# Query products on quarter tiles of TensorE: one head and 64 tokens each, in an attention and Fourier-mix kernel on one core

## The chip, the core and the metric

The kernel runs on one core of a Trainium2 chip. Its five engines work side by side, each with an instruction queue of its own: TensorE multiplies matrices and writes into PSUM banks, VectorE (DVE), ScalarE (ACT) and GpSimd (POOL) work on elements, SyncE (SP) issues transfers. The metric is the device time of the whole program in microseconds. Before the change the median of three runs is 1039.37 us (1037.9 to 1042.61).

## What is computed

Eight batches of 576 tokens, 8 heads of 64 columns. First an attention without a token-by-token matrix, then a Fourier mix with a two-layer network:

```python
q_s = exp(q - max(q, head's columns));  q_s /= sum(q_s, head's columns) + 1e-9
k_s = exp(k - max(k, tokens));          k_s /= sum(k_s, tokens) + 1e-9
kv  = einsum('bhsd,bhse->bhde', k_s, v)          # a 64x64 table a head
x   = einsum('bhsd,bhde->bhse', q_s, kv)         # heads joined to 512 columns
u   = x + real(fft(fft(x, axis=tokens), axis=columns))
out = u + relu(norm(u) @ w_ch1) @ w_ch2          # 512 -> 2048 -> 512
```

The step that matters here is the second product with the table, `q_s` times `kv`. Everything is float32.

## The kernel before

The program is one list of steps, each with a time in a plan made by hand. The steps are sorted by that time and issued in that order, so every engine's queue has a fixed order. A batch's attention is planned among the matmuls of the network of an earlier batch: TensorE works on the network (lines 1371, 1468, 1498, 1587, products with fewer multiplications by Strassen's rule), and now and then takes a few products of the attention.

**Tables.** Heads come in four pairs, `r` = 0 to 3. The table of a pair is kept as one square of 128x128 with the two 64x64 heads on its diagonal and zeros elsewhere, and two further columns P and P+1, one for each head, that hold ones in the rows of that head: 130 columns a pair, in the tile `kvr`. There are two such tiles, for even and odd batches. `keys.scale` (lines 717 to 726) fills the diagonal from the product of keys and values, once a pair; `prepare` (line 652) writes the ones, by four small memsets on GpSimd.

**Own tokens.** Of a batch's 576 tokens, 512 form four tiles of 128. `own_exp` takes the exponential and lays the tile out turned: 128 rows are the columns of a pair of heads, 128 columns are tokens. `own_times_kv` (line 781) multiplies: for each pair of heads the turned queries are the weights (128x128) and the table is streamed (130 columns). Two pairs share a PSUM bank, two banks a tile. The columns P and P+1 of the result are the sums of a head's queries. `inverse` takes their reciprocals, and two multiplications on VectorE, one a bank, divide and move the result to SBUF. There are 24 such tiles in batches 2 to 7.

**Shared tokens.** The other 64 tokens of two batches share one tile, `F`. It is folded along the tokens for the Fourier transform, and `t_times_kv` (line 996) multiplies 128 of its rows by 128 columns of the same tables, four products into one bank, without the sums. ScalarE copies the bank to two places, and three VectorE instructions fold it. There are 6 such tiles in batches 2 to 7.

**Banks.** All these products, those of keys and values (line 716), and the blocks of the transform (lines 1088 to 1116) take PSUM banks in turn from three, with the name `acc`. A product that asks for a bank waits until whoever reads the bank's former content is done.

In batches 0 and 1 the query products are made by other functions, which are left as they are: `q_times_kv` (line 957), and `t_times_kv` as well.

Of the kernel before, what the change touches and what calls it, by code (L numbers as in the profile page):

```python
# [40 lines left out]
F32 = mybir.dt.float32  # L41
# [97 lines left out]
class _Block:  # L139
    def __init__(self, ctx, tc, q, kT, v, w1, w2, ft, cd, out):  # L140
        self.nc, self.tc = tc.nc, tc
        self.q, self.kT, self.v, self.w1, self.w2, self.out = q, kT, v, w1, w2, out
        self.ft_dram, self.cd_dram = ft, cd
        nc = self.nc
        pool = lambda name, **kw: ctx.enter_context(tc.tile_pool(name=name, bufs=1, **kw))
        self.const, self.work, self.small = pool("const"), pool("work"), pool("small")
        self.ps = pool("ps", space=bass.MemoryType.PSUM)
        self.dram = pool("dram", space=bass.MemoryType.DRAM)
        c = self.const
        self.ident = c.tile([P, P], F32, name="ident")  # L150
        make_identity(nc, self.ident[:])
        self.eps = c.tile([P, 1], F32, name="eps")
        nc.gpsimd.memset(self.eps[:], LN_EPS)
        self.kvr = []
        for b in range(2):
            t = c.tile([P, NR, P + 2], F32, name=f"kvr{b}")
            nc.gpsimd.memset(t[:], 0.0)
            self.kvr.append(t)

        self.sn = []  # L160
        for i in range(2):
            t = c.tile([P, NN], F32, name=f"sn{i}")
            nc.gpsimd.memset(t[:], 0.0)
            self.sn.append(t)

        self.ZT = c.tile([P, KT, P], F32, name="ZT")

        self.Zr, self.ZTr = c.tile([P, HD], F32, name="Zr"), c.tile([P, P], F32, name="ZTr")
        for t in (self.Zr, self.ZTr):
            nc.gpsimd.memset(t[:], 0.0)  # L170
        self.kb = c.tile([P, NR, 4, NC * Q], F32, name="kb")
        kb = self.kb[:].rearrange("p r g s -> p (r g s)")
        self.kss = [kb[:, i * NC * P:(i + 1) * NC * P].rearrange("p (c n) -> p c n", n=P) for i in range(NR)]
        self.vt = c.tile([P, NC, 2 * P + 2], F32, name="vt")

        self.T, self.F = c.tile([P, 2 * NR, 4, NT], F32, name="T"), c.tile([P, 2 * NR, P], F32, name="F")
        nc.gpsimd.memset(self.T[:], 0.0)

        self.ones = c.tile([P, NR, H], F32, name="ones")
        nc.gpsimd.memset(self.ones[:], 0.0)  # L180
        for h in range(2):
            nc.gpsimd.memset(self.ones[64 * h:64 * h + 64].rearrange("p r h -> p (r h)")[:, h::H + 2], 1.0)

        self.sign = c.tile([P, 1], F32, name="sign")
        nc.gpsimd.memset(self.sign[:], -1.0)
        nc.gpsimd.memset(self.sign[0:Q + 1], 1.0)
        d = self.dram
        self.w1s = [d.tile([P, 7, HD], F32, tag=f"w1s{p}", name=f"w1s{p}", bufs=1) for p in range(NP)]
        self.w2s = d.tile([7, P, NP, HD], F32, tag="w2s", name="w2s", bufs=1)

        self.w2d = d.tile([P, len(DEEP), GT], F32, tag="w2d", name="w2d", bufs=1)
        self.plan, self.base = [], {}
        for at in range(1, B + 1):
            self.base[at] = len(self.plan)
            self.plan += [self.w1s[p][:].rearrange("p a n -> p (a n)") for pair in PAIRS for p in pair]
            one = lambda m: self.w2s[WB_AT[m]].rearrange("p a n -> p (a n)")
            first = self.first_deep(at)
            self.plan += [one(m) for m in (ORDER if at == 1 else (1, 2) if at == B else (1,))]
            if at > 1:
                for i in range(first, len(DEEP), 4):  # L200
                    self.plan.append(self.w2d[:, i:min(i + 4, len(DEEP)), :].rearrange("p a n -> p (a n)"))
            if at == B:
                self.plan.append(one(4))

        self.big = c.tile([P, 3 * NF * D], F32, name="big")
        self.fifth = self.big[:, 3 * NF * D - 5 * P:3 * NF * D - P].rearrange("p (r n) -> p r n", n=P)
        nc.gpsimd.memset(self.fifth[0:64], 0.0)
        part = lambda i: self.big[:, i * NF * D:(i + 1) * NF * D].rearrange("p (f n) -> p f n", n=D)
        self.w1sb, self.w2sb, self.h0 = part(0), part(1), part(2)
        self.ft = c.tile([P, 4 * NM], F32, name="ft")  # L210
        self.cd = c.tile([P, 5 * QD + 1], F32, name="cd")
        self.xs, self.live, self.stream = {}, {}, {}
        self.turns = 0
        self.eo, self.unT, self.Z = {}, {}, {}
        self.unused = None

        self.later = []

        self.words = [self.work.tile([P, 2, D], F32, tag=n, name="words", bufs=k) for n, k in (("xs", 2), ("x", 4), ("x", 4))]
# [433 lines left out]
    def prepare(self):  # L653


        G = self.nc.gpsimd
        for t in self.kvr:
            for h in range(2):
                G.memset(t[64 * h:64 * h + 64, :, P + h:P + h + 1], 1.0)
        for col in (0, 2 * P + 1):  # L660
            G.memset(self.vt[:, :, col:col + 1], 1.0)
        G.memset(self.vt[3 * Q:, 0:VD, :], 0.0)
# [24 lines left out]
    def keys(self, b, start):  # L687
# [30 lines left out]
        def scale(r):  # L718
            pk = box.pop(r)
            rec = self.small.tile([P, 1], F32, tag="krec", name="krec", bufs=4)  # L720
            at = P * (r % 2)
            V.tensor_scalar(out=rec[:], in0=pk[:, at:at + 1], scalar1=ATT_EPS, scalar2=None, op0=ALU.add)
            V.reciprocal(rec[:], rec[:])
            for h in range(2):
                s, cols = slice(64 * h, 64 * h + 64), slice(64 * h + 1 - r % 2, 64 * h + 65 - r % 2)
                V.tensor_scalar(out=self.kvr[b % 2][s, r, s], in0=pk[s, cols], scalar1=rec[s, 0:1], scalar2=None, op0=ALU.mult)

        steps = [(0.9 * r, lambda r=r: top(r)) for r in range(NR)]
        steps += at(3.6, self.across(lambda: box["m"], 2, 4 * NR)) + at(4.5, self.across(lambda: box["m"], 1, 4 * NR))
# [19 lines left out]
    def own_exp(self, it):  # L749
# [28 lines left out]

        return [(0, top), (0.9, less), (2.7, turn)] + [(3.6 + n / 2, lambda n=n: exps((n, n + 1))) for n in range(0, 16, 2)]

    def own_times_kv(self, it):
        nc, V, (_, b, c, u) = self.nc, self.nc.vector, it
        box = []

        def times():
            q = self.live.pop(it)[0].rearrange("p (r n) -> p r n", r=NR)
            for half in range(2):
                px = self.acc((P, 2 * (P + 2))).rearrange("p (r n) -> p r n", r=2)
                box.append(px)
                for r in range(2):  # L790
                    nc.tensor.matmul(px[:, r, :], lhsT=q[:, 2 * half + r, :], rhs=self.kvr[b % 2][:, 2 * half + r, :],  # L791
                                     start=True, stop=True)

        def inverse():
            rec = self.small.tile([P, 2, 2, 2], F32, tag="qrec", name="qrec", bufs=4)
            for half in range(2):
                V.tensor_scalar(out=rec[:, half], in0=box[half][:, :, P:], scalar1=ATT_EPS, scalar2=None, op0=ALU.add)
            rows = rec[:].rearrange("p a r h -> p (a r h)")
            V.reciprocal(rows, rows)
            box.append(rec)  # L800

        def out(half):
            x = self.xpart(b, c, u)[:, half * HD:(half + 1) * HD].rearrange("p (r h d) -> p r h d", r=2, h=2)
            V.tensor_tensor(out=x, in0=box[half][:, :, 0:P].rearrange("p r (h d) -> p r h d", h=2),
                            in1=box[2][:, half].unsqueeze(3).to_broadcast([P, 2, 2, DH]), op=ALU.mult)

        return [(0, times), (1.5, inverse), (1.6, lambda: out(0)), (1.7, lambda: out(1))]

# [187 lines left out]
    def t_times_kv(self, b):  # L996
# [3 lines left out]
        box = []  # L1000

        def times():
            px = self.acc((P, D))
            for r in range(NR):
                nc.tensor.matmul(px[:, r * P:(r + 1) * P], lhsT=self.F[:, 2 * r + j], rhs=kvr[:, r, 0:P], start=True,
                                 stop=True)
            box.append(px)

        def copies():
            px = box.pop()  # L1010
            g = self.live["g", b] = self.halves()
            nc.scalar.copy(g[:, 0:D], px)
            nc.scalar.copy(self.xshared(b // 2)[part], px[W:])

# [646 lines left out]
def kernel(ctx: ExitStack, tc: tile.TileContext, q, kT, v, w1, w2, ft,  # L1661
# [22 lines left out]
        return steps + at(t + 24 + 1.65 * soon, blk.norm(groups[b]))  # L1684

    fetch, convert = blk.weights()

    after = {}
    for i, place in enumerate(WORDS_AT):
# [42 lines left out]
    for p, dt in zip((3, 7, 2, 0, 1, 6, 4, 5), (34, 42.5, 57.3, 59.3, 61.3, 63.5, 65.5, 68)):  # L1732
        steps += at(t + dt, combined(1, p))
    steps.append((first + 60, blk.prepare))
    own = [("q", 1, c, u) for c in range(2) for u in range(2)]
    for i, it in enumerate(own):
        at_q = t - 15 + 5.5 * i
# [74 lines left out]
```

## Time and profile before

One execution was profiled. Its span is 1038.0 us and its time 1039.82 us.

| | busy, us | share of the span | instructions |
|---|---|---|---|
| TensorE, matmuls | 1023.7 | 99% | 6066 |
| TensorE, weight loads | 888.8 | 86% | 6066 |
| VectorE | 736.4 | 71% | 1452 |
| ScalarE | 496.1 | 48% | 1246 |
| GpSimd | 441.7 | 43% | 448 |

| products that the change touches | records | busy, us | mean of one, ns |
|---|---|---|---|
| own queries with tables, line 791, 128x128 by 130 columns | 192 | 25.9 | 276 |
| shared queries with tables, line 1005, 128x128 by 128 columns (all eight batches) | 64 | 8.5 | 276 |

PE is TensorE's matmuls, PEld its weight loads, which are recorded apart and overlap the matmuls. A float32 product leaves two records of each. The end of a matmul is modelled, so a record is longer than what the product costs when others follow; the difference between the starts of successive ones tells more. Times such as 444.94 are microseconds from the start of the span. An idle time is followed by the instruction that ended it.

### The profile page before, as it was taken

The page shows a single profiled execution, that of the slowest core. Times are in us where ns is not written, and L with a number is a line of the kernel's source. Part 1 is how long each engine was busy: PE and PEld are TensorE (multiplying, and loading weights), DVE is VectorE, ACT ScalarE, POOL GpSimd, SP SyncE. Part 2 cuts the span into 40 slices and gives each one's busy share as a digit, 9 for nine tenths or more (in the row PEclk, how much of TensorE's full clock was granted, in tenths as well). Part 3 has the DMA queues.
Part 4 walks back from the last instruction along what each step waited for, and adds up shares of the span by engine and source line. Part 5 has one row for each costly group of instructions (what it writes and reads, how often), then busy time and mean ns, then how long its engine had stood idle before and what let it go on. Part 6 is the DMA issues. An engine that isn't in the chain of part 4 may idle for free.

```text
span 1038.0 us, 16852 instructions
## 1 busy us (share of the span) xinstructions
PE 1023.7 (99%) x6066; PEld 888.8 (86%) x6066; DVE 736.4 (71%) x1452; ACT 496.1 (48%) x1246; POOL 441.7 (43%) x448
## 2 busy tenths in 40 slices
PE   8999999999999999999999999999999999999998
PEld 7844554888888899889998999989998998999898
DVE  5898888775766877767765787579758744685463
ACT  5674532772359227841765257823782252151200
POOL 3164420356544646554646555474646470030000
PEclk9999999999999999999999999999999999999999
DMA  8777498686999666965768476947654665575464
GB/s 270 248 260 267 170 259 285 195 246 213 324 309 228 198 238 219 242 233 191 275 199 232 180 257 221 250 172 265 212 176 163 242 236 172 221 275 199 178 233 143
DMA packets 114315, 236.02 MB, mean 227 GB/s; under 512 B 23272, under 2 KB 78696, under 8 KB 103608
## 3 DMA queue, kind: packets, MB, share of 16 engines
q1 hardware_dynamic: 113864, 234.42, 69.2%
q8 instruction: 48, 0.79, 0.3%
q14 instruction: 35, 0.29, 0.1%
q10 hardware_dynamic: 288, 0.26, 0.1%
q0 software_dynamic: 80, 0.26, 0.1%
HBM read 199.79 MB, written 39.06 MB: 230 GB/s over the span
## 4 chain that ended last, share of the span: by engine, by line
PE 89%; DVE 5%; DMA 3%; ACT 1%; issue 0%; SPq 0%; POOL 0%; POOLq 0%; DVEq 0%; ACTq 0%
PE bb L1371 15%; PE ba L1371 10%; PE bc L1371 10%; PE bb L1498 10%; PE ba L1498 7%; PE bc L1498 7%; PE bb L1468 5%; PE acc L716 2%; PE bb L1587 2%; PE bc L1308 2%; PE acc L1088 2%; PE acc L791 2%; PE bb L1287 2%; DMA big<-w1s 2%; PE ba L1287 2%; PE bc L1287 2%
## 5 line engine op out<-in xcount | busy, mean ns | idle before, releaser
L1371 PE MATMUL bb<-unT,big 128*128 128x256 f32 x768 | 181.9, 379 | 0.0
L1371 PEld LDWEIGHTS bb<-unT,big 128*128 128x128 f32 x768 | 144.3, 190 | 19.3 <-DVE u L1341 0.5
L1383 ACT ACTIVATE big<-big 128x512 f32<-128x512 f32 x96 | 60.3, 629 | 157.4 <-DVE big L1382 156.4
L1371 PE MATMUL ba<-unT,big 128*128 128x256 f32 x512 | 124.1, 379 | 1.3 <-DMA big<-w1s 1.3
L775 ACT ACTIVATE qT<-q 32x128 f32<-32x128 f32 x384 | 117.9, 307 | 14.1 <-DVE q L765 9.0
L1371 PE MATMUL bc<-unT,big 128*128 128x256 f32 x512 | 121.7, 379 | 0.0
L1371 PEld LDWEIGHTS bc<-unT,big 128*128 128x128 f32 x512 | 96.1, 190 | 13.2 <-DVE big L1382 0.5
L1371 PEld LDWEIGHTS ba<-unT,big 128*128 128x128 f32 x512 | 94.5, 190 | 13.5 <-DMA big<-w1s 1.5
L1341 DVE TENSOR_TENSOR u<-bb,s 128x512 f32<-128x512 f32 x66 | 45.4, 688 | 84.0 <-PE bb L1371 71.0
L1498 PE MATMUL bb<-big 128*128 128x128 f32 x848 | 104.1, 276 | 0.2 <-DVE u L1505 0.2
L1498 PEld LDWEIGHTS bb<-big 128*128 128x128 f32 x848 | 98.9, 192 | 1.1 <-DVE u L1505 0.6
L1221 POOL COPY unT<-unT 32x256 f32<-32x256 f32 x98 | 42.4, 432 | 91.4 <-DVE unT L1213 87.2
L1448 POOL TENSOR_TENSOR x<-x,big 128x512 f32<-128x512 f32 x45 | 59.3, 1333 | 49.2 <-ACT big L1475 19.4
L1498 PE MATMUL ba<-big 128*128 128x128 f32 x640 | 78.0, 275 | 0.0
L1498 PEld LDWEIGHTS ba<-big 128*128 128x128 f32 x640 | 75.2, 192 | 0.7
L1444 DVE TENSOR_TENSOR big<-big 128x512 f32<-128x512 f32 x98 | 73.5, 781 | 0.0
L762 POOL TENSOR_TENSOR q<-q,qm 128x512 f32<-128x512 f32 x24 | 25.8, 1074 | 98.7 <-DVE qm L757 47.2
L1221 ACT COPY unT<-unT 32x256 f32<-32x256 f32 x126 | 50.7, 402 | 30.4 <-DVE unT L1213 28.6
L385 POOL TENSOR_TENSOR big<-big 128x512 f32<-128x512 f32 x24 | 30.4, 1269 | 69.8 <-ACT big L1383 69.8
L1468 PE MATMUL bb<-big 128*128 128x256 f32 x256 | 59.5, 380 | 0.0
L1382 DVE TENSOR_TENSOR big<-bc,u 128x512 f32<-128x512 f32 x64 | 44.0, 687 | 19.4 <-PE bc L1371 18.6
L1468 PEld LDWEIGHTS bb<-big 128*128 128x128 f32 x256 | 48.2, 190 | 8.1 <-DVE big L1382 0.8
(283 smaller groups left out, 2030.0 us busy)
## 6 DMA issues: line engine op xcount, KB each, us to landing
big<-w2d SPq DMA_DIRECT2D x67, 1024.0 KB
big<-w1s SPq DMA_DIRECT2D x64, 896.0 KB
big<-w2s SPq DMA_DIRECT2D x16, 1024.0 KB
big<-in_w_dram SPq DMA_DIRECT2D x21, 512.0 KB
w2d<-big SPq DMA_DIRECT2D x42, 256.0 KB
kb<-in_kT_dram SPq DMA_DIRECT2D x24, 320.0 KB
q<-in_q_dram SPq DMA_DIRECT2D x28, 256.0 KB
vt<-in_v_dram SPq DMA_DIRECT2D x36, 160.0 KB
```

What stands on the lines that cost most here:

```text
L385: e1.tensor_tensor(out=to(4), in0=at(2), in1=at(3), op=ALU.add)
L775: nc.scalar.activation(to[t, i * Q:i * Q + Q], one, ACT.Exp)
L1221: copy(to, of)
L1287: nc.tensor.matmul(ph[:], lhsT=self.w1sb[:, f, k * P:(k + 1) * P], rhs=unT()[:, k // 2 * 2:k // 2 * 2 + 2, k % 2, :], start=(k == 0), stop ...
L1341: plus = lambda t: V.tensor_tensor(out=temp(t), in0=box["bb"][:], in1=box["s1"][:], op=ALU.add)
L1371: nc.tensor.matmul(bank()[:, i, :], lhsT=w[:, WA_AT[m], k * P:(k + 1) * P], rhs=self.unT[g][:, B_AT[m], k, :], start=first and i == 0 and ...
L1382: steps = [(0, lambda: V.tensor_tensor(out=hp(i), in0=bank()[:], in1=u()[:], op=ALU.add)), (0.8, lambda: nc.scalar.activation(hp(i), hp(i) ...
L1383: (0.8, lambda: nc.scalar.activation(hp(i), hp(i), ACT.Relu))]
L1444: e.tensor_tensor(out=to(o), in0=to(x), in1=to(y), op=op)
L1448: E.tensor_tensor(out=x, in0=x, in1=tile(m), op=ALU.add)
L1468: nc.tensor.matmul(box[name][:, i, :], lhsT=h[p][:, A_AT[m], i * P:(i + 1) * P], rhs=self.stream[n][:, p, :], start=p == 0 and (m != 1 or ...
L1498: nc.tensor.matmul(box[place[n]][:, i, :], lhsT=own(m)(A_AT[n])[:, f, :], rhs=w[:, r // 2, r % 2 * P:r % 2 * P + P], start=first and f == ...
```

## The change

Batches 2 to 7 no longer use the squares with zeros. The same memory is viewed as `pairs`: for each of the four pairs of heads 128 rows (64 a head) by 65 columns, the head's table and one column of ones. `keys.scale` writes a head's table to the same 64 columns for both heads. A new function, `by_head`, makes the products: for each pair of heads, each head and each half of the tokens one product of 64 rows (the head's columns) and 64 tokens with 65 streamed columns. Each of the four products of a pair lies on another quarter of TensorE's 128x128 array: rows by head, columns by half of the tokens. The results of head 0 of each pair go into one bank, those of head 1 into another. A tile of queries takes 16 products, before 4.

What reads the results is turned accordingly: the sums are column 64 of each pair, `out` works by head instead of by two pairs. The shared tile takes two banks instead of one, and ScalarE reads it out in four copies instead of two. The ones are one memset of 128 rows for the even batches, in `prepare`; for the odd batches, whose memory batch 1 still uses as a square, another memset is planned later.

```diff
-        self.kvr = []
+        self.kvr, self.pairs = [], []
         for b in range(2):
             t = c.tile([P, NR, P + 2], F32, name=f"kvr{b}")
             nc.gpsimd.memset(t[:], 0.0)
             self.kvr.append(t)
+            self.pairs.append(t[:].rearrange("p r n -> p (r n)")[:, 0:NR * (DH + 1)].rearrange("p (r n) -> p r n", r=NR))
...
-        for t in self.kvr:
-            for h in range(2):
-                G.memset(t[64 * h:64 * h + 64, :, P + h:P + h + 1], 1.0)
+        G.memset(self.pairs[0][:, :, DH:], 1.0)
...
-                V.tensor_scalar(out=self.kvr[b % 2][s, r, s], in0=pk[s, cols], scalar1=rec[s, 0:1], scalar2=None, op0=ALU.mult)
+                V.tensor_scalar(out=self.pairs[b % 2][s, r, 0:DH], in0=pk[s, cols], scalar1=rec[s, 0:1], scalar2=None, op0=ALU.mult)
...
+    def by_head(self, b, left):
+
+        px = [self.acc((P, NR * (DH + 1))).rearrange("p (r n) -> p r n", r=NR) for _ in range(2)]
+        for r in range(NR):
+            for h in range(2):
+                rows = slice(64 * h, 64 * h + 64)
+                for i in range(2):
+                    cols = slice(64 * i, 64 * i + 64)
+                    self.nc.tensor.matmul(px[h][cols, r, :], lhsT=left(r)[rows, cols], rhs=self.pairs[b % 2][rows, r, :],
+                                          start=True, stop=True)
+        return px
...
             q = self.live.pop(it)[0].rearrange("p (r n) -> p r n", r=NR)
-            for half in range(2):
-                px = self.acc((P, 2 * (P + 2))).rearrange("p (r n) -> p r n", r=2)
-                box.append(px)
-                for r in range(2):
-                    nc.tensor.matmul(px[:, r, :], lhsT=q[:, 2 * half + r, :], rhs=self.kvr[b % 2][:, 2 * half + r, :],
-                                     start=True, stop=True)
+            box.extend(self.by_head(b, lambda r: q[:, r, :]))
...
-            for half in range(2):
-                V.tensor_scalar(out=rec[:, half], in0=box[half][:, :, P:], scalar1=ATT_EPS, scalar2=None, op0=ALU.add)
+            for h in range(2):
+                V.tensor_scalar(out=rec[:, h], in0=box[h][:, :, DH], scalar1=ATT_EPS, scalar2=None, op0=ALU.add)
...
-        def out(half):
-            x = self.xpart(b, c, u)[:, half * HD:(half + 1) * HD].rearrange("p (r h d) -> p r h d", r=2, h=2)
-            V.tensor_tensor(out=x, in0=box[half][:, :, 0:P].rearrange("p r (h d) -> p r h d", h=2),
-                            in1=box[2][:, half].unsqueeze(3).to_broadcast([P, 2, 2, DH]), op=ALU.mult)
+        def out(h):
+            x = self.xpart(b, c, u).rearrange("p (r h d) -> p r h d", r=NR, h=2)[:, :, h]
+            V.tensor_tensor(out=x, in0=box[h][:, :, 0:DH], in1=box[2][:, h].unsqueeze(2).to_broadcast([P, NR, DH]),
+                            op=ALU.mult)
...
         def times():
+            if b > 1:
+                box.extend(self.by_head(b, lambda r: self.F[:, 2 * r + j]))
+                return
             px = self.acc((P, D))
...
         def copies():
+            g = self.live["g", b] = self.halves()
+            if b > 1:
+                heads = lambda a, h: a.rearrange("p (r h d) -> p r h d", r=NR, h=2)[:, :, h]
+                for h in range(2):
+                    nc.scalar.copy(heads(g[:, 0:D], h), box[h][:, :, 0:DH])
+                for h in range(2):
+                    nc.scalar.copy(heads(self.xshared(b // 2)[part], h), box[h][W:, :, 0:DH])
+                return
...
+    steps.append((t + 30, lambda: nc_memset(blk.pairs[1][:, :, DH:], 1.0)))
```

More of the change, by code (lines that the diff above doesn't have):

```diff
@@ L786, in times @@
             q = self.live.pop(it)[0].rearrange("p (r n) -> p r n", r=NR)
-            for half in range(2):
-                px = self.acc((P, 2 * (P + 2))).rearrange("p (r n) -> p r n", r=2)
-                box.append(px)
-                for r in range(2):
-                    nc.tensor.matmul(px[:, r, :], lhsT=q[:, 2 * half + r, :], rhs=self.kvr[b % 2][:, 2 * half + r, :],
-                                     start=True, stop=True)
+            box.extend(self.by_head(b, lambda r: q[:, r, :]))
         def inverse():
-            rec = self.small.tile([P, 2, 2, 2], F32, tag="qrec", name="qrec", bufs=4)
-            for half in range(2):
-                V.tensor_scalar(out=rec[:, half], in0=box[half][:, :, P:], scalar1=ATT_EPS, scalar2=None, op0=ALU.add)
-            rows = rec[:].rearrange("p a r h -> p (a r h)")
+            rec = self.small.tile([P, 2, NR], F32, tag="qrec", name="qrec", bufs=4)
+            for h in range(2):
+                V.tensor_scalar(out=rec[:, h], in0=box[h][:, :, DH], scalar1=ATT_EPS, scalar2=None, op0=ALU.add)
+            rows = rec[:].rearrange("p h r -> p (h r)")
             V.reciprocal(rows, rows)
             box.append(rec)
-        def out(half):
-            x = self.xpart(b, c, u)[:, half * HD:(half + 1) * HD].rearrange("p (r h d) -> p r h d", r=2, h=2)
-            V.tensor_tensor(out=x, in0=box[half][:, :, 0:P].rearrange("p r (h d) -> p r h d", h=2),
-                            in1=box[2][:, half].unsqueeze(3).to_broadcast([P, 2, 2, DH]), op=ALU.mult)
+        def out(h):
+            x = self.xpart(b, c, u).rearrange("p (r h d) -> p r h d", r=NR, h=2)[:, :, h]
+            V.tensor_tensor(out=x, in0=box[h][:, :, 0:DH], in1=box[2][:, h].unsqueeze(2).to_broadcast([P, NR, DH]),
+                            op=ALU.mult)
         return [(0, times), (1.5, inverse), (1.6, lambda: out(0)), (1.7, lambda: out(1))]
@@ L1009, in copies @@
         def copies():
+            g = self.live["g", b] = self.halves()
[6 more added lines that the diff above has]
+                return
             px = box.pop()
-            g = self.live["g", b] = self.halves()
             nc.scalar.copy(g[:, 0:D], px)
@@ L1686 @@
     fetch, convert = blk.weights()
+    nc_memset = tc.nc.gpsimd.memset
     after = {}
```

## The prediction

> **What bounds the kernel now.** I read the page first: the busy shares, then the granted clock, then the chain that ended last.
>
> ```profile
> PE 1023.7 (99%) x6066; PEld 888.8 (86%) x6066; DVE 736.4 (71%) x1452; ACT 496.1 (48%) x1246; POOL 441.7 (43%) x448
> ...
> PEclk9999999999999999999999999999999999999999
> ...
> PE 89%; DVE 5%; DMA 3%; ACT 1%; issue 0%; SPq 0%; POOL 0%; POOLq 0%; DVEq 0%; ACTq 0%
> ```
>
> TensorE is busy from end to end at full clock and is 89% of the chain. Its queue is in order, so time that a product gains or loses there passes to the end almost one for one. The question is what one product costs TensorE. The groups of instructions with shapes kept apart give the two lines that change:
>
> ```profile
> L791 PE MATMUL acc<-kvr,qT 128*128 128x130 f32 x192 | 25.9, 276 | 0.4 <-DVE kvr L726 0.4
> L1005 PE MATMUL acc<-kvr,F 128*128 128x128 f32 x64 | 8.5, 276 | 0.4 <-DVE big L374 0.4
> ```
>
> A tile of 128 queries has 4 products, and 192 records for 24 tiles make 8 each: each float32 product is recorded as two pairs of a weight load and a matmul. The mean of 276 ns is a latency, not a cost: matmuls overlap. The cost is from one start to the next, in the timeline of TensorE's matmuls (start, length, line, count):
>
> ```profile
> 444.07 1.03 PE L1371 MATMUL ba<-unT,big 128*128 128x256 f32 x4
> 444.94 1.06 PE L791 MATMUL acc<-kvr,qT 128*128 128x130 f32 x8
> 445.83 0.38 PE L1371 MATMUL ba<-unT,big 128*128 128x256 f32 x1
> ```
>
> From 444.94 to 445.83 is 0.89 us for 8 pairs: 111 ns a pair. The tiles of the shared queries (L1005) take the same: 540.49 to 541.38.
>
> What makes 111? Two things run side by side in a pair: the matmul streams its columns, and the next weights are loaded. The chain in order of time prices the streaming, from long stretches of one shape:
>
> ```profile
> 64.48 3.43 PE bb L1287 x8
> ...
> 195.99 1.73 PE bb L1371 x8
> ```
>
> 512 columns take 3.43/8 = 429 ns, 256 columns 1.73/8 = 216: 0.83 ns a column and 3 ns a pair. The timeline of the weight loads prices the load, where only 8 columns are streamed (L967) and nothing else can set the pace:
>
> ```profile
> 19.21 0.97 PEld L967 LDWEIGHTS bc<-ones,qT 128*128 128x128 f32 x8
> 20.11 0.64 PEld L975 LDWEIGHTS acc<-kvr,qT 128*128 128x128 f32 x5
> ```
>
> 0.90 us for 8 loads: 112 ns for 128 columns of weights. So a pair costs the longer of load and stream, at 130 columns about 111 by either, and the trace shows the loads strictly one after another.
>
> **The change part by part.** *The products.* In 24 own and 6 shared tiles of batches 2 to 7, 4 products (8 pairs) become 16 (32 pairs). 30 tiles at 0.89 go: 26.7 us. A new pair streams 65 columns: 65 x 0.83 + 3 = 57 ns. Its load has 64 columns; half of 112 is 56, if a load scales with its columns. No row has a load of another width than 127 or 128, nor a matmul on part of the array. So the price is bounded by rows: below by four tiles going at once, 8 rounds of 57 = 0.46 us a tile of queries; above by a load that costs 112 ns whatever its width, 32 x 112 = 3.58. Between them lies one pair after another, 32 x 57 = 1.82. I take 1.82: it is what the trace shows of TensorE, each weight load beginning after the one before it, each matmul after its own load. That is +0.93 x 30 = +27.9 us.
>
> *Going over to small tiles and back,* 60 times. No row shows it. Below nothing: it is no work, so no gain. Above: a matmul of 128 columns is recorded with 275 ns while starts are 111 apart, so up to 165 ns of it lie under the next one today; if the array has to run empty at each change, 60 x 0.165 = +9.9. The nearest row is the change from L1371's to L791's shape, which costs nothing (0.87 from 444.07 to 444.94 for four of 216). I take 0 and keep 9.9 for the range. The Trainium skill, TensorEngine Tiling, Key Properties, says that changing the tiling mode drains TensorE; no run here shows it; by that rule the sum below would end near 1076 instead of 1066.
>
> *Waits that longer products cover.* The tile of queries at 338.81 is followed by an idle wait for weights, and the first tile of batches 2 and 3 waits inside for its last table (at 209.35 and 322.60, 1.36 and 1.39 us instead of 0.89, of which the second line below counts only a part):
>
> ```profile
> PE ba L1371 <- DMA big<-w1s: 1.3, 1, 1.3
> ...
> PE acc L791 <- DVE kvr L726: 0.4, 2, 0.2
> ```
>
> The weights come by a transfer that began before four of the lengthened tiles (3.7 us in all), and the last table is now wanted after 24 of 32 pairs, 1.37 us in, when it came at 1.03. All three go: -1.3 - 0.47 - 0.50 = -2.3.
>
> *Banks.* A shared tile now takes two of the three acc banks, before one. Where it follows an own tile directly (222.00, 324.86, 540.49, 760.96), its second bank is the own tile's first, free when VectorE's first multiply ends:
>
> ```profile
> 761.21 0.22 DVE L797 TENSOR_SCALAR qrec<-acc 128x4 f32<-128x4 f32 x2
> 761.46 0.20 DVE L799 RECIPROCAL qrec<-qrec 128x8 f32<-128x8 f32 x1
> 761.70 0.75 DVE L804 TENSOR_TENSOR x<-acc,qrec 128x256 f32<-128x256 f32 x2
> ```
>
> The first of the two ends at 762.1. With products at 1.82 the bank is wanted at 760.96 + 0.93 + 0.11 = 762.0: 0.1 us late. So at 324.86 and 540.49; at 222.00, where no other work lies between the two tiles, about 0.9. Together +1.2. If the products were not longer, the waits would be about 1 us each (0.3 at 324.86), 3.3 in all.
>
> *Nothing on the path.* VectorE's lines 726, 797 and 804 keep count and size (48 each). ScalarE reads a shared tile out in four copies, not two: 4 x 372 ns (line 1098's 128x256 copy) against 584 + 582, +0.3 us a tile, 1.9 in all, under TensorE (ScalarE 48% busy); the first matmul on those rows starts 19 us later (241 after 222), and without that cover it would be 1.9. GpSimd loses four memsets of 99 ns and gains two of about 116; the second stands where GpSimd idles 8 us (126.5 to 134.4), after the last product on the old table (L975, 123.8), and delays nobody. Uncovered: 0.1.
>
> **Sum.** The profiled execution took 1039.82 (span 1038.0 and 1.8 around it; the median of the three is 1039.37, the same within the noise). 1039.8 + 27.9 + 0 - 2.3 + 1.2 = 1066.6.
>
> **The rivals.** *Four tiles at once (faster).* If the array takes the four small products of a round together, loads too, a tile of queries is 8 rounds of 57 = 0.46: -0.43 x 30 = -13. The bank waits then cost 3.3 + 4 x 0.43 = 5, the three covered waits stay: 1039.8 - 13 + 5 = 1032. It decides from 23 ns a pair: below that, 32 pairs and the bank waits fit into 0.89. For it: the four small products use different rows or columns, so nothing forces an order. Against: the two pairs of one product use the same tile and add into the same columns, so they must follow each other, and no row shows a matmul start before the one ahead of it. In the Trainium skill, TensorE: Matmul & The Clock Gate, Part 3 (packing small matmuls), matmuls on different tiles run concurrently with starts about 4 ns apart; no run here shows it, and the speedups told there would be this case.
>
> *Loads go ahead, matmuls stay in order (same).* If a tile's first load runs under the tile before, a product costs its two streams, one of them overlapped: 57 + 3 = 60 ns, 16 x 60 = 0.96 a tile: +0.07 x 30 = +2, bank waits +3.3, covered waits -0.5: 1045; with the arrays emptied, 1055. For it: today's loads already overlap the matmul before. Against: they start only after it has started.
>
> *Loads of fixed length (much slower).* If 64 columns load as slowly as 128, or if the products are not placed on small tiles, 3.58 a tile: +2.69 x 30 = +80.7, -2.3: 1118. For it: every load of these products is 190 ns by record, and none shows a shorter pace than 110. Against: they all have 127 or 128 columns.
>
> **How the numbers follow.** One after another 0.50 (1060 to 1077 by its own bounds); loads ahead 0.22 (1040 to 1056); something between these two, as when only half the changes of tile overlap, 0.08; four at once 0.11; fixed loads 0.09. The predicted time is the first, 1066. From 1036 to 1082 the first three lie inside: 0.80, with four at once and fixed loads left out. Half a per cent, 5.2 us, is about what a measurement of this kernel can tell from no change (its three runs spread over 4.7). Faster by more is four at once: 0.11. Within: the better half of loads ahead and a spoiled four at once, 0.13. Slower: 0.76.
>
> **What would show it.** Right: matmuls on 64x64 with 32 records a tile of queries and starts 57 ns apart, so 1.8 us from the first small product to the next line's first; the waits at 209, 323 and 341 gone; TensorE still 99% busy. An empty array shows as over 57 ns between the last matmul of 128x128 and the first small one. Wrong: starts a few ns apart (four at once), pairs of 57 and 3 in turn (loads ahead), or 112 throughout (fixed loads).

## The result and the profile after

| | median, us | ratio to before, 95% interval |
|---|---|---|
| before (12 runs) | 1039.16 | |
| after (12 runs) | 1040.41 | 1.0016, 1.0008 to 1.0023 |

The change makes the kernel slower by 1.2 us, 0.16%, which twelve runs of each can just tell from nothing. The page of the kernel after:

```profile
span 1037.4 us, 18315 instructions
...
PE 1022.0 (99%) x6786; PEld 875.8 (84%) x6786; DVE 736.4 (71%) x1452; ACT 496.8 (48%) x1258; POOL 441.3 (43%) x446
...
PE 90%; DVE 6%; DMA 2%; ACT 1%; issue 1%; SPq 0%; POOL 0%; POOLq 0%; ACTq 0%
```

TensorE still sets the time. The 720 more matmuls and as many more loads are there (6786 after 6066). The profiled execution took 1039.13, the shortest of the twelve, and it was 2.4 us ahead of the one before when the first changed product came (206.93 against 209.35), by transfers and products that are the same in both programs. About 1 us of that is the clock: in the execution before, TensorE's granted clock was 0.50 of full speed from 9.9 to 13.2, in the one after it was 1.00 there. So the page's shorter span says nothing of the change; the places have to be compared.

The two groups that replace lines 791 and 1005, from the groups of TensorE's matmuls with shapes kept apart:

```profile
L788 PE MATMUL acc<-kvr,qT 64*64 64x65 f32 x768 | 17.8, 224 | 0.1
...
L788 PE MATMUL acc<-kvr,F 64*64 64x65 f32 x192 | 5.4, 225 | 3.0 <-DVE x L810 2.9
```

768 records of own tiles are busy for 17.8 us, where 192 took 25.9. These are times in which at least one of them runs, so they count overlapping products once: the products did become cheaper, not dearer. The timeline of TensorE's matmuls shows one tile of queries in its place, the same tile that was shown of before at 444.94:

```profile
441.28 1.03 PE L1387 MATMUL ba<-unT,big 128*128 128x256 f32 x4
442.23 0.70 PE L788 MATMUL acc<-kvr,qT 64*64 64x65 f32 x32
442.86 0.70 PE L1387 MATMUL ba<-unT,big 128*128 128x256 f32 x2
```

and that of the weight loads:

```profile
441.50 0.41 PEld L1387 LDWEIGHTS ba<-unT,big 128*128 128x128 f32 x2
442.23 0.56 PEld L788 LDWEIGHTS acc<-kvr,qT 64*64 64x64 f32 x32 [0.33 <-issue]
442.86 0.51 PEld L1387 LDWEIGHTS ba<-unT,big 128*128 128x128 f32 x3
```

How fast the 32 follow each other is seen by counting. The answer by windows, for line 788 alone, gives the window's length, the busy time of the matmuls and of the loads, each with, in brackets, how many have begun by the end of the window, and then clock and transfers:

```profile
442.22:442.28 0.06, 0.05 (x4) 0.05 (x4) 1.00 1.09 171
442.22:442.38 0.16, 0.15 (x8) 0.15 (x12) 1.00 1.30 192
442.22:442.44 0.22, 0.21 (x12) 0.21 (x16) 1.00 1.27 191
...
442.22:442.74 0.52, 0.51 (x32) 0.51 (x32) 1.00 1.07 146
```

Four begin together; the next four follow about 0.1 us later, since nothing covers the first loads, and then four more begin every 0.06 us. All four quarters of the array work at once: 8 rounds of 58 to 59 ns, 0.48 us, where my forecast had 32 in a row, 1.82.

The rest is at the edges. Four matmuls of 216 ns from 441.28 would let the next begin at 442.14. The first small load begins at 442.23: 0.09 in which nothing is loaded or streamed, and 0.055 more for a load that nothing covers. At the end the last four of the 32 begin just over 442.69 and stream to 442.77; the load of the next full weights begins at 442.86, another 0.09, and takes 0.11. (The first L1387 matmul is recorded from 442.86, but waits for that load: the two end at 443.56, the second is 0.38 long and began at 443.18, so the first streamed from 442.97.) The tile takes 0.09 + 0.055 + 0.48 + 0.09 + 0.11 = 0.83, from 442.14 to 442.97. Before, it took 0.89. Of 0.41 won by the products 0.34 goes at the edges.

And shared tiles wait for their second bank. TensorE's waits, and the place near 760 in the timelines of TensorE and of VectorE:

```profile
PE acc L788 <- DVE x L810: 2.9, 3, 1.0
```

```profile
758.83 0.33 PE L788 MATMUL acc<-kvr,F 64*64 64x65 f32 x4
760.12 0.69 PE L788 MATMUL acc<-kvr,F 64*64 64x65 f32 x28 [0.95 <-DVE x L810]
```

```profile
759.54 0.76 DVE L810 TENSOR_TENSOR x<-acc,qrec 128x256 f32<-128x256 f32 x2
```

Four records are made, the others begin 1.29 us later, when the first of the two multiplications of the own tile ahead has freed its bank. Measured by the starts, shared tiles hold TensorE for 1.90, 1.09, 1.90 and 1.90 us at 219.18, 323.27, 537.65 and 758.83, where 0.63 is normal (0.57 at 219.18, which follows a small tile; the run with another bank shows it): 4.3 us.

Set against each other by the starts from the first changed tile on: tiles and edges -2.5 us, banks +4.3, the two waits for a last table +0.2, and the wait for weights at 341, which is not there in this execution, -1.5. That is +0.5 of the 1.7 by which the lead shrinks between these two executions, from 2.4 to 0.7 at the end (the medians differ by 1.2). The same alignment shows nine steps of 0.06 to 0.10 us at network matmuls that the change doesn't touch, 0.75 in all, and 0.35 at a product of the transform (357.92 before, 355.28 after). At seven of the nine a weight load now waits 0.21 to 0.26 us for VectorE's line 1398; before, the same loads waited 0.15 or 0.16 or not at all. One of them, in the timeline of the weight loads:

```profile
679.64 0.51 PEld L1387 LDWEIGHTS bc<-unT,big 128*128 128x128 f32 x3 [0.23 <-DVE big L1398]
```

The other two stand at 846.46, where a load waits 0.33 us for a transfer of weights.

### The profile page after: what moved, and what is told of

It reads as the page before. It is cut to its first block, busy times and chain, and to the rows that moved or that the text cites. A ratio compares the mean times of both kernels' runs of the same rounds, so it can differ in the third digit from the quotient of the medians.

```text
span 1037.4 us, 18315 instructions
## 1 busy us (share of the span) xinstructions
PE 1022.0 (99%) x6786; PEld 875.8 (84%) x6786; DVE 736.4 (71%) x1452; ACT 496.8 (48%) x1258; POOL 441.3 (43%) x446
## 4 chain that ended last, share of the span: by engine, by line
PE 90%; DVE 6%; DMA 2%; ACT 1%; issue 1%; SPq 0%; POOL 0%; POOLq 0%; ACTq 0%
PE bb L1387 16%; PE ba L1387 11%; PE bc L1387 10%; PE bb L1514 10%; PE bc L1514 7%; PE ba L1514 7%; PE bb L1484 5%; PE acc L715 2%; PE bb L1603 2%; PE bc L1324 2%; PE acc L1104 2%; PE bb L1303 2%; PE ba L1303 2%; PE bc L1303 2%; PE acc L1107 2%; PE acc L788 2%
## 5 line engine op out<-in xcount | busy, mean ns | idle before, releaser
L1387 PE MATMUL bb<-unT,big 128*128 128x256 f32 x768 | 182.7, 380 | 0.0
L1387 PEld LDWEIGHTS bb<-unT,big 128*128 128x128 f32 x768 | 144.3, 190 | 19.8 <-DVE u L1357 0.5
L1387 PE MATMUL ba<-unT,big 128*128 128x256 f32 x512 | 126.2, 383 | 0.0
L1387 PE MATMUL bc<-unT,big 128*128 128x256 f32 x512 | 122.4, 381 | 0.0
L1387 PEld LDWEIGHTS bc<-unT,big 128*128 128x128 f32 x512 | 96.0, 190 | 14.0 <-DVE big L1398 1.4
L1387 PEld LDWEIGHTS ba<-unT,big 128*128 128x128 f32 x512 | 94.5, 190 | 13.5 <-issue 0.5
```

The costliest lines, as they stand in the source:

```text
L1387: nc.tensor.matmul(bank()[:, i, :], lhsT=w[:, WA_AT[m], k * P:(k + 1) * P], rhs=self.unT[g][:, B_AT[m], k, :], start=first and i == 0 and ...
```

## The experiments

Ratios are to the kernel before, run beside each version; medians of different versions come from different chips in part. One theory and two rivals stood after the result. The theory: small products run four at once, each going over to small tiles and back costs 0.34 us, and banks cost the rest. The rivals: the edges are a start-up of the products themselves and not of the change of shape, or the real loss lies on another engine.

### Another bank

```diff
-        px = [self.acc((P, NR * (DH + 1))).rearrange("p (r n) -> p r n", r=NR) for _ in range(2)]
+        flat = self.turned().rearrange("p r n -> p (r n)")[:, 0:NR * (DH + 1)]
+        px = [t.rearrange("p (r n) -> p r n", r=NR) for t in (self.acc((P, NR * (DH + 1))), flat)]
```

> A tile's second result bank comes from the two banks of the turned tiles (tr), which stand idle in batches 2 to 7, instead of from the three of acc; the products and their order stay. Theory (small products run four at once, and what they gain goes into going over to small tiles and back and into bank waits): in the trace of the changed kernel four shared tiles hold TensorE for 1.90, 1.09, 1.90 and 1.90 us where an undisturbed one takes 0.63 (0.52 when another small tile stands ahead), 4.4 us in all. They go: about 1040.4 - 4.4 = 1036, 0.997 of the time before. Rival (the bank waits only hide another wait behind them, on VectorE or a transfer): 1039 to 1041.

Measured: 1037.93 us, 0.9990 (0.9978 to 1.0003), 2.5 us under the kernel after. In the trace every shared tile now takes 0.63, or 0.57 behind another small tile, so 4.3 us are gone there. But 1.4 of them come back as a wait for weights at 341, which the profile of before had and that of after had not (TensorE's waits):

```profile
PE ba L1388 <- DMA big<-w1s: 1.6, 2, 1.3
```

The banks of `tr` are not quite idle in these batches (in the profile of before, eight records of line 913 write them between 419 and 641), but no wait for them shows. The theory has its place right, and the rival has a part: another wait stood behind. Whether the kernel after is without it because the banks hold TensorE up at 323, or because the transfer was quicker in that one execution, one profile of each can't tell.

### The same products in two visits

`by_head` gets two more arguments, the banks and the pairs of heads to make; that part is left out here:

```diff
         def times():
-            q = self.live.pop(it)[0].rearrange("p (r n) -> p r n", r=NR)
-            box.extend(self.by_head(b, lambda r: q[:, r, :]))
+            q = self.live[it][0].rearrange("p (r n) -> p r n", r=NR)
+            box.extend(self.by_head(b, lambda r: q[:, r, :], None, (0, 1)))
+
+        def times_more():
+            q = self.live.pop(it)[0].rearrange("p (r n) -> p r n", r=NR)
+            self.by_head(b, lambda r: q[:, r, :], box[0:2], (2, 3))
...
-        return [(0, times), (1.5, inverse), (1.6, lambda: out(0)), (1.7, lambda: out(1))]
+        return [(0, times), (0.9, times_more), (1.5, inverse), (1.6, lambda: out(0)), (1.7, lambda: out(1))]
```

> As e1_banks, but the products of each own tile are made in two visits, pairs of heads 0 and 1 first, 2 and 3 some 0.8 us later, with products of the network between them. TensorE then goes over to small tiles 46 times instead of 29. Theory (each going over and back costs 0.34 us: 0.09 of empty array and 0.055 for the first small load on the way in, 0.09 and 0.108 for the full load on the way out): 17 x 0.34 = +5.9 us above e1_banks, about 1042. Rival (the gaps at the edges are a start-up cost of a tile's first products and not of the change of shape, or go by the record only): within 1 us of e1_banks.

Measured: 1.0052 (1.0032 to 1.0071) against 0.9990: +6.4 us for 17 more visits, 0.38 each; the medians say 5.5, 0.32 each. No product was added. The trace says it without the scatter of the runs: from the first start to the next line's, a whole tile takes 0.63 and half a tile 0.39, and each visit loses 0.2 more at its neighbours, so two halves cost 2 x 0.59 = 1.18 where one visit costs 0.83, 0.35 more. The cost is the change of shape, paid at each visit.

### Neighbours on the same quarter

```diff
-        for r in range(NR):
-            for h in range(2):
-                rows = slice(64 * h, 64 * h + 64)
-                for i in range(2):
-                    cols = slice(64 * i, 64 * i + 64)
+        for h in range(2):
+            rows = slice(64 * h, 64 * h + 64)
+            for i in range(2):
+                cols = slice(64 * i, 64 * i + 64)
+                for r in range(NR):
```

> The changed kernel with another order of the 16 small products: the four pairs of heads of one quarter of the array directly after each other, then the next quarter, so neighbours share a quarter three times in four. Theory (TensorE runs small products side by side only as neighbours on different quarters): 32 pairs of 57 ns, 1.82 us a tile of queries instead of 0.48, +1.34 x 30 less the bank waits that this covers (about 3): 1075 to 1080. Rival (TensorE picks any product of its queue whose quarter is free): about 1040, as the changed kernel.

Measured, in two runs: 1059.7 us, 1.0194 (1.0165 to 1.0223): between the two. The answer by windows for line 788, counted as above:

```profile
442.78:442.88 0.10, 0.09 (x1) 0.10 (x2) 1.00 1.19 205
442.78:442.94 0.16, 0.15 (x2) 0.15 (x3) 1.00 1.18 196
...
442.78:443.06 0.28, 0.27 (x4) 0.28 (x5) 1.00 1.21 203
442.78:443.12 0.34, 0.33 (x6) 0.34 (x7) 1.00 1.21 205
```

On one quarter a pair begins every 58 ns, the price that my forecast gave to all. From the fifth on the next quarter's pairs come in beside them. So TensorE looks ahead, but only some three pairs far: the last three of a quarter's eight are shared with the next quarter, three times. 32 x 57 - 9 x 57 = 1.31, and 0.34 at the edges: 1.65, and the trace has 1.67 a tile (1.47 from the first start to the next line's, and 0.2 that the neighbours lose). Both theories of this run were too simple: it is neither neighbours alone nor any product of the queue. How TensorE picks, the records do not say; the reach of three pairs is what they show here.

### Halves instead of quarters

By rows of the array:

```diff
-                for i in range(2):
-                    cols = slice(64 * i, 64 * i + 64)
-                    self.nc.tensor.matmul(px[h][cols, r, :], lhsT=left(r)[rows, cols], rhs=self.pairs[b % 2][rows, r, :],
-                                          start=True, stop=True)
+                self.nc.tensor.matmul(px[h][:, r, :], lhsT=left(r)[rows, :], rhs=self.pairs[b % 2][rows, r, :],
+                                      start=True, stop=True)
```

> The changed kernel with half as many products of twice the width: 64 rows (one head), all 128 tokens as weights, 65 columns streamed, so the array is cut by rows alone and two products can run side by side. Theory (a round lasts as long as the longer of a quarter's load and stream, loads of the two halves side by side, and the change of shape costs the same): 16 pairs, two at a time, 8 rounds of 112 ns (the load of 128 columns) and 0.34: 1.24 us a tile instead of 0.83, +0.41 x 29, less 2 of bank waits: about 1050. Rival 1 (loads of the two halves one after another): 16 x 112 and 0.34 = 2.1 us, about 1077. Rival 2 (cutting by rows needs no emptying): 0.9 to 1.0 us, 1041 to 1044.

and by columns, in the kernel before:

```diff
                 for r in range(2):
-                    nc.tensor.matmul(px[:, r, :], lhsT=q[:, 2 * half + r, :], rhs=self.kvr[b % 2][:, 2 * half + r, :],
-                                     start=True, stop=True)
+                    for i in range(2):
+                        s = slice(64 * i, 64 * i + 64)
+                        nc.tensor.matmul(px[s, r, :], lhsT=q[:, 2 * half + r, s], rhs=self.kvr[b % 2][:, 2 * half + r, :],
+                                         start=True, stop=True)
```

> The kernel before, with each product of the 24 own tiles cut by columns of the array alone: all 128 rows, 64 tokens as weights, the table's 130 columns streamed, twice as many products. Theory (two halves run side by side, a round is the stream of 130 columns, 111 ns, and the change of shape costs 0.34 as for quarters): 8 x 0.111 + 0.34 = 1.23 us a tile instead of 0.89, 24 x 0.34 = +8, about 1047. Rival 1 (the halves do not run side by side): 16 x 0.111 + 0.34, +30, about 1069. Rival 2 (a cut by columns needs no emptying): about as before.

Measured: 1052.3 us, 1.0118 (1.0093 to 1.0144), and 1046.7 us, 1.0068 (1.0052 to 1.0083), near the 1050 and 1047 that were expected. Two of the four runs by rows, 1053.4 and 1054.1, are slower than the others, 1050.3 and 1051.2; the trace is of the first, and in it the granted clock is 0.50 from 222.8 to 226.1, which costs 1.7 us. The timeline of TensorE's matmuls by rows:

```profile
434.58 0.59 PE L1385 MATMUL ba<-unT,big 128*128 128x256 f32 x2
435.10 1.11 PE L786 MATMUL acc<-kvr,qT 64*128 64x65 f32 x16
436.14 0.48 PE L1385 MATMUL bb<-unT,big 128*128 128x256 f32 x1
```

and by columns:

```profile
431.37 0.59 PE L1373 MATMUL ba<-unT,big 128*128 128x256 f32 x2
431.90 1.11 PE L793 MATMUL acc<-kvr,qT 128*64 128x130 f32 x16
432.94 0.70 PE L1373 MATMUL bb<-unT,big 128*128 128x256 f32 x2
```

In both 16 records take 1.04 us from the first start to the next line's: eight rounds of two. By rows a round lasts as long as the load of 128 columns, by columns as long as the stream of 130. With 0.2 lost by the neighbours this is the 1.24 us and 1.23 us a tile that was expected, and 0.34 of it is edge. Each of these cuts of the array pays for the change of shape; a round costs the longer of its load and its stream; and loads of different parts run side by side, by rows as by columns.

### One small product

```diff
-                px = self.acc((P, 2 * (P + 2))).rearrange("p (r n) -> p r n", r=2)
+                full = self.acc((P, D))
+                px = full[:, 0:2 * (P + 2)].rearrange("p (r n) -> p r n", r=2)
                 box.append(px)
+                if half:
+                    rows = slice(0, DH)
+                    nc.tensor.matmul(full[rows, 2 * (P + 2):2 * (P + 2) + DH + 1], lhsT=q[rows, 0, rows],
+                                     rhs=self.kvr[b % 2][rows, 0, 0:DH + 1], start=True, stop=True)
```

> The kernel before, with one extra product on a quarter of the array (64 rows, 64 tokens, 65 columns) in each of the 24 own tiles, between its two banks; its result is not read. It measures the change of shape by itself: the product's own streams are 2 x 57 ns. Theory (going over and back costs 0.34 us, less what the covered loads share): 24 x (0.34 + 0.11) = +11 us, about 1050. Rival (no emptying: 24 x 0.11): +2.7, about 1042.

Measured: 1.0089 (1.0073 to 1.0104), +9.2 us, 0.39 for each of 24. TensorE's matmuls around one:

```profile
216.66 0.61 PE L796 MATMUL acc<-kvr,qT 128*128 128x130 f32 x4
217.20 0.33 PE L793 MATMUL acc<-kvr,qT 64*64 64x65 f32 x2
217.46 0.71 PE L796 MATMUL acc<-kvr,qT 128*128 128x130 f32 x4
218.01 0.81 PE L1376 MATMUL ba<-unT,big 128*128 128x256 f32 x3
```

From 216.66 to 218.01 it takes 1.35 us instead of 0.89. Of these 0.46 the product's two streams are 0.11. 24 x 0.46 would be 11; but the wait for weights near 341, 1.3 us before, is not there in this trace, as my prediction had said of longer tiles, and that takes part of it back. A product of 64x64 that comes alone between full ones costs four times its own time; the rival's 2.7 us is out of the interval.

### Fewer visits

The small products of two tiles in one visit, on top of the other bank; the tile that waits is held back until the next one's place in the plan:

```diff
-            steps += at(t, self.own_exp(it)) + at(t + 15, self.own_times_kv(it))
+            steps += at(t, self.own_exp(it))
+        to = {0: 1, 2: 3} if start < 0 else {1: 2} if tail else {2: 3}
+        late = [places[to[n]] if n in to else t for n, t in enumerate(places)]
+        if start == 0 and not tail:
+            late[0] = 14
+        for t, it in zip(late, own):
+            steps += at(t + 15, self.own_times_kv(it))
...
-        return steps + at((33 if start < 0 else 39) if tail else max(22, start + 29), self.t_times_kv(b))
+        return steps + at((33 if start < 0 else places[3] + 15) if tail else max(22, start + 29), self.t_times_kv(b))
```

> As e1_banks, and the small products of two tiles of queries are made in one visit where their plan allows it (own tiles 1 and 2, and 3 and 4, of batches 4 to 7; own 3 and 4, and own 1 with the shared tile, of batch 3; own 2 and 3, and own 4 with the shared tile, of batch 2). TensorE goes over to small tiles 18 times instead of 29. Theory (0.34 us for each going over and back): 11 x 0.34 = 3.8 us under e1_banks, about 1034, 0.995 of the time before; the wait for weights near 340 us takes back up to 0.7 of it: 0.995 to 0.996. Rival (the products themselves set the cost): as e1_banks, 0.999.

Measured: 1037.8 us, 0.9977 (0.9968 to 0.9986). Against the other bank alone that is 1.3 us by the ratios and 0.1 by the medians, where some 3 to 4 were expected, and the intervals overlap. By the starts each pair of batches 4 to 7 wins the 0.35 us it should. But in batches 2 and 3 TensorE waits (the profiled execution, 1041.0, is the slowest of eleven):

```profile
PE ba L1394 <- DMA big<-w1s: 2.9, 2, 2.7
PE bb L1394 <- DVE u L1364: 2.4, 1, 2.4
...
PE ba L1394 <- ACT big L1401: 1.6, 1, 1.6
```

Behind the 2.7 us near 341 more is lost. The answer by windows gives busy times of TensorE's matmuls and loads and of the other engines, and then the granted clock:

```profile
343.80:347.10 3.30, 3.22 (x8) 2.60 (x9) 0.00 (x0) 0.59 (x1) 3.22 (x3) 0.50 1.02 355
```

For 3.4 us from the end of this wait the clock was half, and matmuls of 256 columns begin every 0.43 us instead of 0.216: 1.6 us more. The wait of 2.4 us in the same trace has no such stretch behind it.

Two more versions take the waits apart. The first moves four loads of keys behind two loads of network weights:

```diff
-        steps = at(20 if b == 2 else 27 if b < 5 else 24, self.keys_to(b))
+        steps = at(20 if b == 2 else 27 if b == 3 else 33 if b == 4 else 24, self.keys_to(b))
```

> As e5_pairs, and the four loads of batch 4's keys are issued behind two loads of network weights instead of among them. Theory (the wait of 1.3 us before the weights' arrival near 340 us is real in all versions, and was only covered in the changed kernel by the bank waits that stood ahead of it): the wait goes, 1 to 2 us under e5_pairs, about 1032.5, 0.994. Rival (those weights are late for another reason): as e5_pairs.

Measured: 1036.3 us, 0.9965 (0.9952 to 0.9979), above the 1032.5 that was expected. The wait for weights is gone from the trace, the two others stay, and this time 3.4 us at a clock of 0.50 stand behind the wait of 2.4 us, from 232.5 to 235.9; the gain over the version ahead of it is 1.5 us by the medians, but the intervals overlap. The second has that move too, and pairs tiles in batches 4 to 7 alone:

```diff
-            steps += at(t, self.own_exp(it)) + at(t + 15, self.own_times_kv(it))
+            steps += at(t, self.own_exp(it))
+        late = [places[n + 1] if start < 0 and n in (0, 2) else t for n, t in enumerate(places)]
+        for t, it in zip(late, own):
+            steps += at(t + 15, self.own_times_kv(it))
```

> As e8_pairs_keys, but tiles are paired in batches 4 to 7 alone (21 visits of TensorE to small tiles, 29 in e1_banks). In e5_pairs and e8_pairs_keys the pairs of batches 2 and 3 brought TensorE two new waits, 2.4 us behind VectorE near 230 and 1.6 us behind ScalarE near 341, since a tile held back keeps one of three buffers of turned queries. Theory: both go, three visits more cost 1.0: 3 us under e8_pairs_keys, about 1033.5, 0.994 of the time before. Rival (those waits have another cause): 1036 to 1037.

Measured: 1034.4 us, 0.9956 (0.9943 to 0.9970) of the time before. TensorE's three longest waits lie ahead of the first changed tile; then come 1.1 us in five pieces. The granted clock is full from 7.2 us to 0.7 us before the end.

```profile
PE ba L244 <- POOL kvr L157: 2.3, 1, 2.3
PE acc L1108 <- issue: 1.7, 1, 1.7
PE tr L1216 <- ACT eo L1210: 1.2, 1, 1.2
PE bc L1391 <- DVE big L1402: 1.1, 5, 0.4
```

This version is under both kernels, by 4.3 us and 6.0 us of the medians. That the two waits came from the held-back tile's buffer is not shown by itself: only that they go when tiles of batches 2 and 3 are not held back, and with them the stretch at half clock.

## Where the prediction was right and wrong

I had 1066 us; 1040.4 was measured. My range of 1036 to 1082 holds it, by luck: the sum behind 1066 has its largest term wrong, and the range was drawn for other cases. Put right term by term, the sum is 1039.8 - 30 x 0.41 for products + 9.9 for edges + 4.3 for banks - 1.3 for the covered waits = 1040.4. The small waits of some 1.1 us that the alignment shows are not in it, so the agreement to a tenth is chance.

- **The products: the step that failed.** I priced a tile at 32 x 57 = 1.82 because the trace of before has loads and matmuls one after another. It has them so where each uses the whole array. The trace of after has four together, 0.48. The evidence could not decide this, and I read the absence of an overlap, where none could be, as a sign against one. The reason I held against four at once, that the two pairs of one product must follow each other, fits the run with neighbours on one quarter (a pair every 58 ns) and costs nothing: the other quarters fill the time. The price of 57 ns for a pair was right (58 to 59 measured), for four of them. The Trainium skill, TensorE: Matmul & The Clock Gate, Part 3, had this as a rule, and the trace agrees: four starts within 0.06 us, some 7 ns apart where that page has about 4.
- **Going over and back: the second step that failed.** I took 0 by the nearest row, a change of columns streamed, which isn't a change of shape of the array. Measured are 0.34 us a visit, 29 visits: 9.9 us. That equals my upper bound by coincidence, since it is made of other pieces: 0.09 us with nothing running each way, not 0.165, and the loads that nothing covers, 0.055 and 0.11. The Trainium skill, TensorEngine Tiling, Key Properties, states the draining without a price; the runs agree, for cuts by rows, by columns and by both.
- **Banks: right place, and the right size in the rival.** With quick products I had 5 us at the four places; 4.3 were measured there.
- **Covered waits.** The two waits for a last table were not covered, since products became quicker: about 0.6 us each, as against 0.5 before. The wait for weights at 341 was absent, but not for my reason, since no tile was longer except by a bank wait.
- **The rival of four at once** came out at 1032. With the 9.9 of its own upper bound, which I had put to my forecast and not to it, it is 1042, within 2 us of the measurement. Every bound should have been carried to every case.
- **Nothing on the path:** ScalarE's and GpSimd's extra work stayed off it (48% and 43% busy, as before), and VectorE's busy time is unchanged at 736.4. But the quicker TensorE now meets VectorE at the seven small waits above, about 0.55 us that no term of my sum had.

## What to carry to other kernels

Small products on parts of TensorE's array do run side by side, at the longer of load and stream for a whole round, if neighbours in the queue use different parts. But each visit to another shape costs about 0.34 us here, as much as three pairs of a full load and a matmul of 128 columns, one and a half float32 products: gather small products into few long visits, and count visits before counting products. A second result bank for such products must be free when the visit begins, or its wait eats what the products win.

## What the runs showed of the hardware

The edge of a visit is four pieces: 0.09 us with nothing running, the first small load (0.055), 0.09 again and the first full load (0.11). Quarters and column halves show the same four; by row halves the first load, of 128 columns, is part of the first round, and the stream of the last round, 0.055 too, takes its place. So the sum is 0.34 for all three cuts. Where products of one quarter follow each other, TensorE reaches ahead by about three pairs of a load and a matmul, so an order of products that alternates quarters is worth 19 us here against one that doesn't (1040.4 against 1059.7). Loads of different parts of the array run side by side too: all 32 had begun within 0.52 us, where one after another, at 0.055, they would take 1.76. And a wait of TensorE can be followed by 3.4 us at half the granted clock (behind 2.7 us at 341 and, in another version, 2.4 us at 230), though the wait of 2.4 us was not in every trace.
